# The start of the second layer's second job, the choice of its largest expert, and the turning of relu's values by halves

## The chip, the cores and the metric

The kernel runs on one core of one Trainium2 chip. The metric is device time in microseconds (us) of one execution, the median of several; lower is better.

## The reference

A retention attention over 1536 tokens (2 batches x 768) of 512 features is followed by two mixture-of-experts layers of 8 experts each, all in float32. The attention is not touched by the change. What the two layers compute, cut to what matters:

```python
# layer 1: noisy top-2 gating
noisy = x @ w_gate + log1p(exp(x @ w_noise)) * noise
top2, top2_w = two largest, softmax over them
out[mask] += top2_w[mask, k, None] * (np.maximum(x[mask] @ w1[e], 0.0) @ w2[e])

# layer 2: top-1 gating with a capacity of 384 tokens for each expert
logits = x @ w_gate
expert_idx = np.argmax(logits, axis=1)
gate_w = softmax(logits)[token, expert_idx]
# the first 384 tokens of an expert, in token order, are kept; others give 0
out[i] = gate_w[i] * (np.maximum(x[i] @ w1[e], 0.0) @ w2[e])
```

In both layers w1 is 512 x 1024 and w2 is 1024 x 512 for each expert.

## The kernel before

**Jobs.** The work of a layer is cut into jobs. A job is a set of token rows for one expert: the rows are gathered from memory by an indirect DMA on GpSimd's queue, transposed on TensorE, multiplied by w1, passed through relu, multiplied by w2, weighted and scattered. Layer 1 has two jobs begun ahead and then seven jobs of 372 to 408 rows. Layer 2 has job S (AHEAD, 256 rows of the largest expert, chosen while the last job of layer 1 still runs, from the tokens that job does not hold), job T (BEHIND, 128 more rows of the same expert, with S's weights), and then seven jobs, each for the expert of some rank by size, in the order TURNS = (336, 128, 324, 128, 164, 152, 128 rows). "Job 2" below is the first of these, with 336 rows in three gathers.

**Arithmetic.** Each product is made of three matmuls on high and low parts (`three`, L754 to L756). The weights' high part is cast by ScalarE (L106), the low part subtracted by VectorE (L112). Rows arrive as pairs that GpSimd adds (`both`, L514); TensorE transposes them (L744), ScalarE casts the high part (L745) and VectorE subtracts the low part (L746).

**Steps of a job.** `Job.steps` gives a list of steps. A wide job has nine: first product of one eighth of the hidden features (`first`, 12 matmuls) together with the second product of the eighth before (`second`, 12 matmuls; 6 in S). A job of one 128-row tile works "by token" and has four: `first_rows(0)` and `first_rows(1)` (24 matmuls each, of 128 x 256), whose relu goes to a tile `hr` (ScalarE, L843); `turn(0)` and `turn(1)`, in which TensorE transposes `hr` back, four 128 x 128 pieces each (L850), ScalarE copies the high part (L853) and VectorE subtracts the low part (L854); then `second` in two steps. Five jobs work by token: one of layer 1's first two, T, and the three of 128 rows in layer 2.

**Routing of layer 2.** `ahead` chooses the largest expert: logits are loaded (L1203) and added (L1206), ranked on TensorE (`ranks_of`, L300 and L303), and S's rows are found (`one_hot`, L374 to L387). While S runs, `extra2` routes the rest: `route2` and `one_hot("D", ...)` for T's rows; `others` (sizes, weight loads, and `slots`: `mark` writes twelve 128 x 128 comparisons on VectorE, L451, and `head` multiplies them on TensorE, L458, to give `Tsrc`, the rows of all seven later jobs); `gates` (softmax weights into `aux2`, L1300 to L1313 by way of `split3`, L309 to L313); then the products that bring each row its weight: `jobS.rest` and `jobT.rest` (24 matmuls at L377, copies L379, small transposes L382) and `later[1][7]` (12 matmuls at L458). `sizes_by_expert` and `leftovers` (L991 to L1002) count tokens that no job holds; a branch (L1391) reads that count.

**Order.** `experts` walks jobs and steps and calls `extra(j, i)` after step i of job j. Each engine executes its instructions in one order; `tc.issue_after(x)` keeps what is issued inside behind instruction x, and `tail["pe"]`, `tail["act"]` and `tail["dve"]` hold the latest of an engine. In between the scheduler places instructions by its own estimate. An instruction that waits holds all behind it on its engine. In `experts`, `last.collect()` and `last.finish()` (results of the job before, with its scatters on GpSimd) come after step 0 of a job.

Of the kernel before, what the change touches and what calls it, by code (L numbers as in the profile page):

```python
# [20 lines left out]
P = 128  # L21
# [5 lines left out]
AHEAD, BEHIND = (256, 2), (128, 1)  # L27
# [10 lines left out]
def kernel(ctx: ExitStack, tc: tile.TileContext, q, k, v, lam, g1, gn, noise,  # L38
                                  w1, w2, g2, u1, u2, capacity, out):
    nc = tc.nc  # L40
# [717 lines left out]
    class Job:  # L758
        def __init__(self, key, size, select, source, target, first_layer, wide=False, ranked=False):
            self.key, (self.n, self.nt), self.select = key, size, select  # L760
            self.ranked = ranked
            self.rows = P if ranked else self.n // self.nt
            self.source, self.target, self.first_layer = source, target, first_layer
            self.by_token = self.nt == 1
            self.wide = wide or self.nt > 2
            self.pairs = self.wide and 2 * self.n <= 512
            self.keeps = False
            self.g = self.logits = None
            self.yT = None
            self.apart = not first_layer  # L770
            self.h = {}
# [19 lines left out]
        def steps(self):  # L791
            if self.by_token:
                return [lambda: self.first_rows(0), lambda: self.first_rows(1),
                        lambda: (self.turn(0), self.turn(1), self.second(range(0, 4))),
                        lambda: self.second(range(4, FC))]
            return [lambda: self.first(0)] + [
                (lambda f: lambda: (self.first(f + 1) if f + 1 < FC else None, self.second((f,))))(f)
                for f in range(FC)]
# [34 lines left out]
        def first_rows(self, m):  # L833
            r = self.rows
            ps = bank("hp", [P, 512])[:r]
            for jj in range(2):
                for d in range(DC):
                    w = w1_part(self.key, 2 * m + jj, d, slice(0, 256))
                    three(ps[:, jj * 256:(jj + 1) * 256], (self.x[:, d, 0, :r], self.x[:, d, 1, :r]), w,
                          d == 0, d == DC - 1)  # L840
            used[0] += 2
            hr = work.tile([P, 512], F32, name="hr")
            nc.scalar.activation(hr[:r], ps, AF.Relu)  # L843
            self.h["r", m] = hr

        def turn(self, m):
            r = self.rows
            ps = bank("tr", [P, 4, P])[:, :, :r]
            for i in range(4):
                nc.tensor.transpose(ps[:, i, :], self.h["r", m][:r, i * P:(i + 1) * P], ident[:r, :r])  # L850
            t = work.tile([P, 2, 512], F32R, name="h", bufs=3).rearrange("p a (b c) -> p a b c", b=4)[:, :, :, :r]
            hh, hl = t[:, 0], t[:, 1]
            nc.scalar.copy(hh, ps)  # L853
            nc.vector.tensor_sub(hl, ps, hh.bitcast(F32))  # L854
            for i in range(4):
                self.h[4 * m + i] = t[:, :, i, :]
# [91 lines left out]
    def experts(jobs, last, extra=None, count=None, between=None, joins=3):  # L948

        j = 0  # L950
        while j < len(jobs) and j != count:
            job = jobs[j]
            steps = job.steps()
            for i, step in enumerate(steps):
# [3 lines left out]
                nxt = jobs[j + 1] if j + 1 < len(jobs) else None  # L958
                if i == len(steps) - 1 and j + 1 < len(jobs) and j + 1 != count:
                    job.collect()  # L960
                if i == 0 and last is not None:
                    last.collect()
                    last.finish()
                    if j == 0 and between is not None:
                        between()
# [176 lines left out]
    def extra1(j, i):  # L1142
# [14 lines left out]
        if j == len(FIRST) + 1:  # L1157
            if i == 0:
                final()
            if i == 2:  # L1160
                tokens_of(jobs[j])
                load_logits()
            if i == 4:
                last_logits(lgp)
                first_max(lgp, mm, mb2, sl)
                nc.vector.tensor_mul(mb2[:, sl], mb2[:, sl], whole[:, :, None].to_broadcast(full))
                ahead()
# [107 lines left out]
    keyB, keys, gate = (small(x, [P, NT]) for x in ("keyB", "keys", "gate"))  # L1275
    oo, mB = mb2[:, sl], mb1[:, sl]
    jobT = Job(("b", "s"), BEHIND, None, x2_rows, out, False)
    jobs = [jobS, jobT]
    entered2, regs, later = [], [], []
    tot2 = cnt2[:, NT, :]  # L1280
# [67 lines left out]
    def extra2(j, i):  # L1348
# [5 lines left out]
            later.append(picked)  # L1354
        if j == 0 and i == 3:
            with tc.issue_after(later[0]):
                rk2 = others()
                later.append(rk2)
                of, _, pick, spread1, mark, head = later[1][:6]
                pick()  # L1360
                spread1()
                mark(range(NT))
                later.append(head())
                for k, r in enumerate(TURNS):
                    jobs.append(Job(("b", r), SECOND[r], of(r), x2_rows, out, False, SECOND[r][1] > 1, True))
                jobs[2].prepare()
        if j == 0 and i == 4:
            st2 = sizes_by_expert("b", later[2], [n for n, _ in SECOND] + [BEHIND[0]])
            later.append(leftovers("b", tab2, table2_full, tot2, st2, x2_rows, u1, u2, out, False))

        if j == 0 and i == 5:
            with tc.issue_after(later[3]):
                gates()
            with tc.issue_after(tail["pe"]):
                jobS.rest()
                jobT.rest()
                later[1][6]()
                later[1][7]()
            places.append(more[2])

    jobL = last
    last = experts(jobs, jobL, extra2, count=BEFORE + 2, between=lambda: all_logits(jobL))
# [47 lines left out]
```

## Time and profile before

| what | us |
|---|---|
| median of 3 runs | 632.45 |
| the three runs | 632.22, 632.45, 636.45 |
| the profiled execution's own time | 632.51 |
| its span, first to last instruction | 630.8 |
| TensorE busy | 598.5 |
| VectorE busy | 373.1 |
| ScalarE busy | 279.8 |
| GpSimd busy | 180.1 |

The trace gives a start and a duration for each instruction. In its timeline a row may stand for several like instructions in turn (x3); a bracket at the end of a row tells how long the engine sat idle before it and which instruction, on which engine and line, ended that. Matmuls overlap, so what one costs is read from the distance of the starts. The attention fills the first 92 us, layer 1 goes on to about 423 us, S begins there, T stands at 461 us and job 2 at 476 us. L numbers are lines of the kernel before.

### The profile page before, as it was taken

The page shows a single profiled execution, that of the slowest core. Times are in us where ns is not written, and L with a number is a line of the kernel's source. Part 1 is how long each engine was busy: PE and PEld are TensorE (multiplying, and loading weights), DVE is VectorE, ACT ScalarE, POOL GpSimd, SP SyncE. Part 2 cuts the span into 40 slices and gives each one's busy share as a digit, 9 for nine tenths or more (in the row PEclk, how much of TensorE's full clock was granted, in tenths as well). Part 3 has the DMA queues.
Part 4 walks back from the last instruction along what each step waited for, and adds up shares of the span by engine and source line. Part 5 has one row for each costly group of instructions (what it writes and reads, how often), then busy time and mean ns, then how long its engine had stood idle before and what let it go on. Part 6 is the DMA issues. An engine that isn't in the chain of part 4 may idle for free. (4 is left out here: it accounts for less than half of the span.)

```text
span 630.8 us, 11323 instructions
## 1 busy us (share of the span) xinstructions
PE 598.5 (95%) x4173; PEld 558.7 (89%) x4173; DVE 373.1 (59%) x841; ACT 279.8 (44%) x486; POOL 180.1 (29%) x255
## 2 busy tenths in 40 slices
PE   3999989999999999999999999989899999998896
PEld 3888878989999999999999999978679989987795
DVE  3365769857454363554745535447859568557881
ACT  2466622146353353443534334145037367466771
POOL 3953730274022040120500101032255135132101
PEclk9999999999999999999999999999999999999999
DMA  6799721577645375476532511272597877767620
GB/s 151 156 302 266 186 82 44 168 215 254 203 144 170 109 232 151 136 221 200 193 113 100 177 44 55 60 251 85 171 324 239 277 240 259 248 201 246 214 75 34
DMA packets 106048, 110.34 MB, mean 175 GB/s; under 512 B 35855, under 2 KB 81951, under 8 KB 105984
## 3 DMA queue, kind: packets, MB, share of 16 engines
q1 hardware_dynamic: 97920, 83.58, 43.9%
q0 software_dynamic: 8064, 25.95, 12.2%
q8 instruction: 35, 0.57, 0.4%
q14 instruction: 29, 0.24, 0.1%
HBM read 92.48 MB, written 18.79 MB: 176 GB/s over the span
## 5 line engine op out<-in xcount | busy, mean ns | idle before, releaser
L112 DVE TENSOR_TENSOR wl<-wst,wh 128x1024 fp32r<-128x1024 f32 x107 | 135.2, 1270 | 59.0 <-ACT wh L106 58.6
L106 ACT CAST wh<-wst 128x1024 fp32r<-128x1024 f32 x107 | 111.3, 1047 | 33.4 <-PE yp L755 26.5
L754 PE MATMUL hp<-x,wh 128*128 128x372 f32 (+9 forms) x352 | 116.1, 330 | 0.8 <-ACTq L1264 0.4
L755 PE MATMUL hp<-x,wh 128*128 128x372 f32 (+9 forms) x352 | 116.1, 330 | 0.0
L756 PE MATMUL hp<-x,wl 128*128 128x372 f32 (+9 forms) x352 | 115.3, 328 | 0.0
L828 ACT ACTIVATE h<-hp 128x372 fp32r<-128x372 f32 (+9 forms) x88 | 41.2, 469 | 154.7 <-PE hp L756 151.6
L754 PE MATMUL yp<-h,wh 128*128 128x372 f32 (+8 forms) x320 | 106.9, 334 | 0.0
L756 PE MATMUL yp<-h,wl 128*128 128x372 f32 (+8 forms) x320 | 106.3, 332 | 0.0
L755 PE MATMUL yp<-h,wh 128*128 128x372 f32 (+8 forms) x320 | 105.8, 331 | 0.0
L829 DVE SCALAR_TENSOR_TENSOR h<-hp,h 128x372 fp32r<-128x372 f32 (+9 forms) x88 | 46.4, 527 | 62.9 <-ACT h L828 62.6
L754 PEld LDWEIGHTS hp<-x,wh 128*128 128x128 f32 x352 | 66.1, 188 | 1.9 <-ACTq L1264 0.7
L755 PEld LDWEIGHTS hp<-x,wh 128*128 128x128 f32 x352 | 66.2, 188 | 0.4
L756 PEld LDWEIGHTS hp<-x,wl 128*128 128x128 f32 x352 | 66.1, 188 | 0.1
L504 POOL DMA_INDIRECT xg<-x,Rsrc x25 | 26.4, 1057 | 136.0 <-PE tr L744 118.8
L755 PEld LDWEIGHTS yp<-h,wh 128*128 128x128 f32 x320 | 60.2, 188 | 0.6 <-DVE h L829 0.4
L756 PEld LDWEIGHTS yp<-h,wl 128*128 128x128 f32 x320 | 60.2, 188 | 0.2 <-issue 0.2
L754 PEld LDWEIGHTS yp<-h,wh 128*128 128x128 f32 x320 | 60.2, 188 | 0.0
L746 DVE TENSOR_TENSOR x<-tr,x 128x128 fp32r<-128x128 f32 (+12 forms) x72 | 29.2, 436 | 38.0 <-ACT x L745 37.5
L941 POOL DMA_INDIRECT x<-y,Rdst x25 | 25.0, 1000 | 80.9 <-DVE y L915 78.5
L745 ACT CAST x<-tr 128x128 fp32r<-128x128 f32 (+12 forms) x72 | 25.9, 387 | 41.3 <-PE tr L744 40.8
L514 POOL TENSOR_TENSOR xg<-xg 128x512 f32<-128x512 f32 (+1 forms) x16 | 24.7, 1546 | 39.3 <-DMA xg<-x,Tsrc 24.4
L906 PE MATMUL tr<-iw,yT 128*128 128x136 f32 (+2 forms) x224 | 34.2, 287 | 0.0
(370 smaller groups left out, 1029.3 us busy)
## 6 DMA issues: line engine op xcount, KB each, us to landing
wst<-in_moe_w_dram SPq DMA_DIRECT2D x107, 512.0 KB, 4.8
more<-in_moe_w_dram SPq DMA_DIRECT2D x21, 512.0 KB, 5.3
ldk<-in_k_dram SPq DMA_DIRECT2D x12, 256.0 KB, 5.5
ldq<-in_q_dram SPq DMA_DIRECT2D x6, 512.0 KB, 6.2
ldv<-in_v_dram SPq DMA_DIRECT2D x12, 256.0 KB, 6.0
x<-xr SPq DMA_DIRECT2D x12, 256.0 KB, 2.9
out_dram<-zero SPq DMA_DIRECT2D x12, 256.0 KB, 4.9
dm<-powers SPq DMA_DIRECT2D x1, 512.0 KB, 5.4
```

Of the source, the lines that this page charges most:

```text
L106: nc.scalar.copy(hi, st)
L112: nc.vector.tensor_sub(lo, st, hi.bitcast(F32))
L504: i = nc.gpsimd.indirect_dma_start(out=r, out_offset=None, in_=x, in_offset=bass.IndirectOffsetOnAxis(ap=src(s)[:m], axis=0))
L745: a = nc.scalar.copy(hi[:, d, :n], ps[:, :n])
L746: v_ = nc.vector.tensor_sub(lo[:, d, :n], ps[:, :n], hi[:, d, :n].bitcast(F32))
L754: nc.tensor.matmul(ps, a[0], b[0], start=start, stop=False)
L755: nc.tensor.matmul(ps, a[0], b[1], start=False, stop=False)
L756: tail["pe"] = nc.tensor.matmul(ps, a[1], b[0], start=False, stop=stop).ins
L828: tail["act"] = nc.scalar.activation(hh, ps, AF.Relu).ins
L829: tail["dve"] = nc.vector.scalar_tensor_tensor(hl, ps, 0.0, hh.bitcast(F32), op0=OP.max, op1=OP.subtract).ins
L906: nc.tensor.matmul(ps[:m, i, :], self.yT[:, 2 * b + i, s * r:s * r + m], iw[:, 2 * b + i, gates2], start=True, stop=True)
L941: i = nc.gpsimd.indirect_dma_start(out=target, out_offset=bass.IndirectOffsetOnAxis(ap=dst, axis=0), in_=y, in_offset=None, bounds_check=t ...
```

## The change

Three things are moved; TensorE's number of instructions stays as it was.

- In the last job of layer 1, the logits' sum, `first_max` and `ahead` come after step 3 instead of step 4.
- At layer 2's start, `head` of the later jobs' rows and the gather of job 2 come after S's step 7 instead of step 3. The gates come after them (step 7 instead of 5), the weights' products after T's step 0, sizes and leftovers after T's step 1. S's results are collected and scattered after T's step 1 (`clears = 1`).
- In a job by token, `turn(0)`'s transposes stand in the middle of `first_rows(1)`, and `turn(1)`'s after the first two of `second`'s eight parts.

```diff
         def steps(self):
             if self.by_token:
                 return [lambda: self.first_rows(0), lambda: self.first_rows(1),
-                        lambda: (self.turn(0), self.turn(1), self.second(range(0, 4))),
+                        lambda: (self.second(range(0, 2)), self.turn(1, tail["pe"]), self.second(range(2, 4))),
                         lambda: self.second(range(4, FC))]
...
             for jj in range(2):
+                if m and jj:
+                    self.turn(0, tail["pe"])
                 for d in range(DC):
...
-        def turn(self, m):
+        def turn(self, m, ahead):
             r = self.rows
             ps = bank("tr", [P, 4, P])[:, :, :r]
-            for i in range(4):
-                nc.tensor.transpose(ps[:, i, :], self.h["r", m][:r, i * P:(i + 1) * P], ident[:r, :r])
+            with tc.issue_after(ahead):
+                for i in range(4):
+                    nc.tensor.transpose(ps[:, i, :], self.h["r", m][:r, i * P:(i + 1) * P], ident[:r, :r])
...
-                if i == 0 and last is not None:
+                if i == job.clears and last is not None:
                     last.collect()
                     last.finish()
...
-            if i == 4:
+            if i == 3:
                 last_logits(lgp)
                 first_max(lgp, mm, mb2, sl)
...
+    jobT.clears = 1
...
         if j == 0 and i == 3:
             with tc.issue_after(later[0]):
-                rk2 = others()
-                later.append(rk2)
-                of, _, pick, spread1, mark, head = later[1][:6]
+                later.append(others())
+                of, _, pick, spread1, mark = later[1][:5]
                 pick()
                 spread1()
                 mark(range(NT))
-                later.append(head())
-                for k, r in enumerate(TURNS):
-                    jobs.append(Job(("b", r), SECOND[r], of(r), x2_rows, out, False, SECOND[r][1] > 1, True))
+        if j == 0 and i == 7:
+            with tc.issue_after(tail["pe"]):
+                later.append(later[1][5]())
+                for r in TURNS:
+                    jobs.append(Job(("b", r), SECOND[r], later[1][0](r), x2_rows, out, False, SECOND[r][1] > 1, True))
                 jobs[2].prepare()
-        if j == 0 and i == 4:
-            st2 = sizes_by_expert("b", later[2], [n for n, _ in SECOND] + [BEHIND[0]])
-            later.append(leftovers("b", tab2, table2_full, tot2, st2, x2_rows, u1, u2, out, False))
-
-        if j == 0 and i == 5:
-            with tc.issue_after(later[3]):
+        if j == 0 and i == 7:
+            with tc.issue_after(later[3]), tc.issue_after(tail["dve"]):
                 gates()
+                later[1][6]()
+        if j == 1 and i == 0:
             with tc.issue_after(tail["pe"]):
                 jobS.rest()
                 jobT.rest()
-                later[1][6]()
                 later[1][7]()
             places.append(more[2])
+        if j == 1 and i == 1:
+            with tc.issue_after(tail["dve"]):
+                st2 = sizes_by_expert("b", later[2], [n for n, _ in SECOND] + [BEHIND[0]])
+                later.append(leftovers("b", tab2, table2_full, tot2, st2, x2_rows, u1, u2, out, False))
```

TensorE's order in the middle of T, before (`hr` is relu's output, `hp` the first product's and `yp` the second product's bank, `iw` holds the identity matrix):

```order
L756 MATMUL hp<-wh_79,x_1224 128x256
L850 MATMUL tr<-iw,hr 128x128 x8
L754 MATMUL yp_5330<-wh_80,h 128x512
L755 MATMUL yp_5330<-wl_88,h 128x512
L756 MATMUL yp_5330<-wh_80,h 128x512
L754 MATMUL yp_5330<-wh_80,h 128x512
L755 MATMUL yp_5330<-wl_88,h 128x512
L756 MATMUL yp_5330<-wh_80,h 128x512
```

and of the change, the two places where four transposes each stand now:

```order
L756 MATMUL hp<-wh_78,x_1224 128x256
L854 MATMUL tr<-iw,hr 128x128 x4
L754 MATMUL hp<-wh_79,x_1224 128x256
...
L754 MATMUL yp_5322<-wh_80,h 128x512
L755 MATMUL yp_5322<-wl_88,h 128x512
L756 MATMUL yp_5322<-wh_80,h 128x512
L854 MATMUL tr<-iw,hr 128x128 x4
L754 MATMUL yp_5322<-wh_81,h 128x512
L755 MATMUL yp_5322<-wl_89,h 128x512
```

The eight transposes that stood together between the two products are now four among the first product's matmuls, twelve ahead of its end, and four behind six matmuls of the second. All five jobs by token have this order.

VectorE's order around the change from S to T, before (`Tsrc` are the later jobs' rows, `aux` the gates' split values, `tabi` the copy of the weights' products):

```order
L472 TENSOR_SCALAR Tsrc<-slt 128x21
L475 SCALAR_TENSOR_TENSOR Tdst<-slt,sld 128x21
L996 TENSOR_REDUCE blw<-ovs 128x8
...
L313 CAST aux_152<-sp_r 128x12
L446 TENSOR_TENSOR yT<-yT,aux_152 128x756
L379 COPY tabi<-tr 4x256
L383 COPY Soa<-tr 128x2x4
```

and of the change (`wl` is the low part of job 2's weights):

```order
L472 TENSOR_SCALAR Tsrc<-slt 128x21
L475 SCALAR_TENSOR_TENSOR Tdst<-slt,sld 128x21
L1305 TENSOR_REDUCE keeps<-keep 128x12
...
L313 CAST aux_152<-sp_r 128x12
L112 TENSOR_TENSOR wl_84<-wst_73,wh_76 128x1024
L446 TENSOR_TENSOR yT<-yT,aux_152 128x756
L112 TENSOR_TENSOR wl_85<-wst_74,wh_77 128x1024
L379 COPY tabi<-tr 4x256
```

Two conversions of job 2's weights now stand between the gates and the first copy of the weights' products.

GpSimd's order from the gather of T's rows on, before (`Dsrc` are T's rows, `Tsrc` those of job 2 and later, `Sdst` where S's results go):

```order
L504 DMA xg<-x_67,Tsrc 128x1104 x2
L504 DMA xg<-x_67,Tsrc 80x1104
L514 TENSOR_TENSOR xg<-xg 128x4x128 x2
L941 DMA out_dram<-y,Sdst 1536x512 x2
L514 TENSOR_TENSOR xg<-xg 80x4x128
L504 DMA xg<-x_67,Tsrc 128x1104
```

and of the change:

```order
L504 DMA xg<-x_67,Tsrc 128x1104 x2
L504 DMA xg<-x_67,Tsrc 80x1104
L514 TENSOR_TENSOR xg<-xg 128x4x128 x2
L504 DMA xg<-x_67,Tsrc 128x1104
L514 TENSOR_TENSOR xg<-xg 80x4x128
L945 DMA out_dram<-y,Sdst 1536x512 x2
```

The third addition for job 2 and the first gather for the job after it stand ahead of S's two scatters now.

## Rows read from the trace of the kernel before

**Rows 1.** Page, busy time, share of the span and instructions of each engine

```profile
PE 598.5 (95%) x4173; PEld 558.7 (89%) x4173; DVE 373.1 (59%) x841; ACT 279.8 (44%) x486; POOL 180.1 (29%) x255
```

**Rows 2.** Waits of TensorE over the span: sum in us, times, longest

```profile
PE tr L850 <- ACT hr L843: 1.3, 5, 0.3
```

**Rows 3.** Timeline, TensorE, 417 to 421 us: start, duration, instruction, idle before and releaser

```profile
417.79 0.33 PE L756 MATMUL yp<-h,wl 128*128 128x372 f32 x1
418.33 0.33 PE L744 MATMUL tr<-iw,xg 128*128 128x128 f32 x1 [0.22 <-POOL xg L514]
420.21 0.55 PE L744 MATMUL tr<-iw,xg 128*128 128x128 f32 x3 [1.54 <-POOLq L1264]
420.51 0.41 PE L754 MATMUL yp<-h,wh 128*128 128x372 f32 x1
```

**Rows 4.** Timeline, GpSimd, the second addition for S's rows

```profile
418.89 1.26 POOL L514 TENSOR_TENSOR xg<-xg 128x512 f32<-128x512 f32 x1 [0.61 <-DMA xg<-x,Ssrc]
```

**Rows 5.** Timeline, VectorE, two steps' relu and the logits, 389 to 398 us

```profile
389.63 0.55 DVE L829 SCALAR_TENSOR_TENSOR h<-hp,h 128x372 fp32r<-128x372 f32 x1 [0.56 <-ACT h L828]
393.71 0.55 DVE L829 SCALAR_TENSOR_TENSOR h<-hp,h 128x372 fp32r<-128x372 f32 x1 [3.54 <-ACT h L828]
396.10 0.26 DVE L1206 TENSOR_TENSOR lgp<-lg 128x96 f32<-128x96 f32 x1 [1.84 <-DMA lg<-x]
...
397.85 0.26 DVE L1166 TENSOR_TENSOR mb<-mb,whole 128x96 bf16<-128x96 bf16 x1
```

**Rows 6.** Timeline, TensorE, the ranks for the largest expert

```profile
403.21 0.22 PE L300 MATMUL tr<-mb,tri 128*128 128x104 bf16 x1
```

**Rows 7.** Timeline, TensorE, from S to T's first matmul

```profile
453.32 0.47 PE L458 MATMUL yp<-yT,more 128*128 128x42 bf16 x12 [1.60 <-DVE more L451]
...
455.87 0.73 PE L756 MATMUL yp<-wh,h 128*128 128x512 f32 x2 [0.42 <-DVE h L829]
457.82 1.47 PE L377 MATMUL tr<-oh,aux 128*4 128x256 bf16 x12 [1.23 <-DVE aux L313]
...
461.72 0.39 PE L754 MATMUL hp<-wh,x 128*128 128x256 f32 x1 [0.40 <-ACT x L745]
```

**Rows 8.** Tile `more`, group of the marks' comparisons: duration ns min/median/max, first and last start

```profile
L451 DVE TENSOR_SCALAR more<-slot,yT x36: 242/245/1352, 114.1 to 453.0; 128x128 bf16<-128x128 f16 x36
```

**Rows 9.** Timeline, GpSimd, additions for T's rows and job 2's second and third gather

```profile
451.79 1.26 POOL L514 TENSOR_TENSOR xg<-xg 128x512 f32<-128x512 f32 x1 [3.78 <-DMA xg<-x,Dsrc]
...
465.57 1.99 POOL L514 TENSOR_TENSOR xg<-xg 128x512 f32<-128x512 f32 x1 [1.32 <-DMA xg<-x,Tsrc]
...
470.85 1.32 POOL L514 TENSOR_TENSOR xg<-xg 80x512 f32<-80x512 f32 x1
```

**Rows 10.** Timeline, TensorE, T's turn and the start of its second product

```profile
467.78 0.28 PE L756 MATMUL hp<-wh,x 128*128 128x256 f32 x1
467.90 0.60 PE L850 MATMUL tr<-iw,hr 128*128 128x128 f32 x4
...
470.29 0.40 PE L754 MATMUL yp<-wh,h 128*128 128x512 f32 x1
...
472.35 0.74 PE L744 MATMUL tr<-iw,xg 128*128 128x128 f32 x6
...
473.21 0.40 PE L755 MATMUL yp<-wl,h 128*128 128x512 f32 x1
```

**Rows 11.** Timeline, ScalarE, the turned values' copy in T

```profile
469.50 0.59 ACT L853 CAST h<-tr 128x512 fp32r<-128x512 f32 x1 [0.32 <-PE tr L850]
```

**Rows 12.** Timeline, VectorE, the turned values' low part in T

```profile
470.12 0.69 DVE L854 TENSOR_TENSOR h<-tr,h 128x512 fp32r<-128x512 f32 x1 [0.21 <-ACT h L853]
```

**Rows 13.** Page, costliest groups: busy us, mean ns, idle before and what ended it

```profile
L112 DVE TENSOR_TENSOR wl<-wst,wh 128x1024 fp32r<-128x1024 f32 x107 | 135.2, 1270 | 59.0 <-ACT wh L106 58.6
L106 ACT CAST wh<-wst 128x1024 fp32r<-128x1024 f32 x107 | 111.3, 1047 | 33.4 <-PE yp L755 26.5
```

**Rows 14.** Windows: us, busy of PE, PEld, DVE, ACT, POOL, PEclk, DMA share, GB/s

```profile
455.00:460.00 5.00, 3.35 (x28) 2.06 (x27) 3.89 (x15) 0.28 (x1) 2.84 (x3) 1.00 1.07 380
```

More of the change, by code (lines that the diff above doesn't have):

```diff
@@ L767, in __init__ @@
             self.keeps = False
+            self.clears = 0
             self.g = self.logits = None
```

## The prediction

> **What bounds the kernel now.** I read the page's busy times first. TensorE is busy for 598.5 of 630.8 us [rows 1]; no other engine comes near. So the time is TensorE's work plus the moments at which it has nothing to do, and an edit is worth what it takes from either. The second view is the list of TensorE's waits: most are outside the reach of this change, and the ones within reach are few. Its row for the turn of relu's values is 1.3 us in five times [rows 2], one for each job by token. The others I take from TensorE's timeline, where a bracket shows what ended a wait: 0.22 and 1.54 us before the transposes of S's rows [rows 3]; then 1.60 us for the marks, 0.42 for the low part of relu, 1.23 for the gates' last split value and 0.40 for T's rows, all between S and T [rows 7]. After them I read the other engines at those moments, to see what would come late if TensorE came sooner.
>
> The sum is made in the profiled execution: it took 632.51 us, 1.71 more than its span, and the median is 632.45, so no correction is needed.
>
> **Choosing sooner.** From the last matmul before S's transposes to the first one behind them is 420.51 - 417.79 = 2.72 us [rows 3]. One matmul's place there is about 0.17 (a step of 24 matmuls takes 393.71 - 389.63 = 4.08 us [rows 5]), and four transposes cost about 0.46 (worked out under the turn). So 2.1 us are lost, and the 1.54 of them ends when GpSimd's second addition ends, at 418.89 + 1.26 = 420.15 [rows 4]. The choice comes one step, 4.08 us, sooner, so this addition would end at 416.1, ahead of TensorE at about 418. Is there data for it? The logits land at 396.1, the marks of the largest are there at 397.85 + 0.26 = 398.1 [rows 5], and TensorE ranks them only at 403.21 [rows 6]; a step sooner is 399.1, 1.0 us after. The cover is 1.0 us: if it went, VectorE would hold TensorE's ranks for the rest. All that ahead() issues moves with it, S's gathers and weight loads too; GpSimd and the load queue have nothing else there. A conversion of S's weights comes before the branch instead of after, which is ScalarE's and VectorE's time. I take 1.85 us (2.1 less some 0.25 for transposes of the last job's results that now stand closer); bounds 0 and 2.1.
>
> **The start of T.** TensorE's work is the same, so I count waits. Gone from where they are: 1.60 + 0.42 + 1.23 + 0.40 = 3.65 us [rows 7]. What is late next:
> - The marks. TensorE now comes to their products six matmuls after relu instead of four, and with two transposes of T's rows between: some 0.7 us later. VectorE does the marks behind less other work, but one of them took 1.352 us instead of 0.245 [rows 8] at the time of GpSimd's addition for T (451.79, 1.26 us [rows 9]), and that meeting stays. I leave 0.2 of the 1.60; bounds 0 and 0.9.
> - The gates. T's first product starts where the old waits and the products at L377 and L458 are not: these fill 461.72 - 0.40 - 457.82 = 3.5 us, so it starts near 461.72 - 3.65 - 3.5 + 0.5 = 455.1 on the old clock (0.5 for T's own transposes), and its 24 matmuls of 0.12 us (467.90 - 467.78 [rows 10]) end at 458.0. The gates' last value is there at 457.8 before [rows 7]. I take 0.3, in case of delays by the memsets and counts of the leftovers that stand among the gates now; bounds 0 and 1.
> - The copy of the weights' products (L379). It now stands behind two conversions of job 2's weights, 1.27 us each [rows 13], which themselves wait for casts of 1.05. TensorE has the 12 products at L458 (0.47 for such a group [rows 7]) and seven matmuls of 0.12 between, 1.3 us. I take 0.25; bounds 0 and 2.5, the two conversions whole.
>
> That is 3.65 - 0.75 = 2.9 us. Then T's end: TensorE comes sooner to the transposes of job 2's rows. Before, they stand at 472.35 [rows 10], and GpSimd's third addition ends at 470.85 + 1.32 = 472.17 [rows 9]: they are just in time. The change puts this addition ahead of S's scatters (it could follow the second, 465.57 + 1.99 = 467.56 [rows 9], and end near 468.9). TensorE's new time is 472.35 - 2.9 - 0.76 (T's turn, below) = 468.7. So it is just in time again: I take a wait of 0.3, bounds 0 and 1.8 (one addition of 1.99 instead of 1.28 or so, and one more blocked). Sum of this part: 2.6 us, bounds -1.8 and 3.65.
>
> The slow mark stands in a rule: the Trainium skill, "SBUF — State Buffer", section "Who interferes with whom", says that VectorE and GpSimd share a port pair that one instruction holds whole, so that the other blocks until it is done; the trace agrees in one case, by 1.352 - 0.245 = 1.1 us, near the 1.26 of the addition. It speaks against the change: additions for job 2 meet conversions with two inputs in memory. If each of its three additions cost the later engine one such 1.1 us on the path, the sum would be lower by 3.3; I keep the bounds above, since most conversions don't hold TensorE.
>
> **The turn.** Before, eight transposes stand together, TensorE waits 0.26 for the second relu (1.3 us in five [rows 2]), and the second product's third matmul waits for the low part. From 467.90 to the fourth matmul at 470.29 is 2.39 us [rows 10]; three matmuls at 0.229 (nine from 470.29 to 472.35 [rows 10]) are 0.69, so the turn costs 1.70. Among matmuls, six transposes cost 473.21 - 472.35 - 0.229 = 0.63 [rows 10]; I take 0.47 for four, so 0.94 for both halves. A job saves 0.76, and five jobs 3.8 us. What hides the copies: after the first four transposes, 12 matmuls of 0.12 and two of the second product, 1.44 + 0.46 = 1.9 us, stand before the low part is wanted. The copy takes 0.59 [rows 11] and the subtraction 0.69, and VectorE waited 0.21 before it [rows 12]; twice that for the passing between engines makes 1.7. It is covered by little. A conversion of 1.05 on ScalarE stands just ahead of the copy [rows 13], in place of the wait. I take off 0.05 a job: 3.55 in all; bounds 1.5 (0.45 a job lost) and 3.9.
>
> **Sum.** 1.85 + 2.6 + 3.55 = 8.0 us; 632.5 - 8.0 = 624.5 us. All parts at their good end give 2.1 + 3.65 + 3.9 = 9.65, so 622.8; lower still, 622, if transfers that start sooner also shorten waits after T.
>
> **Rivals.**
> 1. GpSimd or its transfers become the new wait at job 2. For it: a DMA share of 1.07 at 455 to 460 us [rows 14], when these gathers are on their way: the 16 engines are full, so rows can't come sooner. Against it: the queue of additions is shorter by two scatters. Then TensorE waits about 1.8 us at job 2 and the neighbour's conversions lose 0.5: 624.5 + 2.3 = 626.8.
> 2. The weights' products only move their waits: VectorE's two conversions ahead of L379 hold TensorE for 2.5 us, and part two is worth 0.35. For it: the order; against it: TensorE's 1.3 us of other work, half of the two conversions. Time 624.5 + 2.25 = 626.75.
> 3. The choice isn't sooner where it counts, since the logits' transfer (the 1.84 us wait ending at 396.10 [rows 5]) decides. For it: that wait; against it: 1.0 us of margin. Time 624.5 + 1.85 = 626.35.
> 4. Slower: ScalarE. The copy of the first half stands behind a cast of weights that must have landed; before, the transposes came later by the whole of 1.4 us. If the casts of the next job's weights wait for their load, TensorE stops in the middle of each job by token. It decides where a load comes over 2 us late in each of the five: at 2 us the turn's 3.55 becomes 3.55 - 10 and the time 634.5. For it: the full DMA engines [rows 14]; against it: the casts' idle time is nearly all put down to TensorE's use of the slots (26.5 of 33.4 us), not to a transfer [rows 13].
>
> **How the numbers follow.** Forecast 0.60, rival 1 0.15, rival 2 0.12, rival 3 0.07, rival 4 0.06. A measurement of this kernel can tell about 1% (6.3 us) from no change. Below 626.1 lies the forecast's case but for a tenth of it, and half of rivals 1 to 3, whose times are within a microsecond of that line: 0.54 + 0.17 = 0.71, less a little for two at once: 0.68. Within 1% the rest, but 0.03 for the part of rival 4 beyond 638.8. The range goes from 622.0 to 628.0, which takes in rivals 1 to 3 with a second small loss, and leaves out rival 4 and sums of several.
>
> **What would show it.** In the changed profile, S's four transposes should have no wait of over 0.3 us, and the last addition for S should end before 416. Between S and T's first matmul there should be one wait of under 1 us, and waits at L377, L382 and L458 of under 1 us together. No wait of TensorE for `hr`; T's second product begins after 24 + 24 matmuls without a gap, and job 2's first matmul stands near 471 us. If the waits between 450 and 470 add up to over 3 us, part two was wrong; if the wait at L744 for GpSimd is over 1.5 us, rival 1; if the second product waits for the low part by over 0.3 us in each job by token, the turn's cover was too thin; if the relu of the steps at 390 to 400 us comes late, rival 3.

## The result and the profile after

The changed kernel took 624.59 us (median of 4 runs, 623.98 to 626.13), the kernel before 632.71 beside it: a ratio of 0.9876, 95% interval 0.9853 to 0.9899. That is 8.1 us less; 8.0 were forecast, and 624.5 as the time. The sum came out right, but not all of its terms did, and that they cancelled to 0.1 us is luck. The profiled execution was the longest of the four (626.13 us, span 624.4), and why it was is part of the story.

The table gives the stages of three profiles as distances, in us, between the starts of TensorE's first matmuls. The third column is a second profile of the changed kernel (run f1 below).

| from the first matmul of ... to ... | before | changed | changed, second profile |
|---|---|---|---|
| layer 1 to the job behind its job by token | 50.42 | 49.63 | 49.69 |
| that job to S | 278.60 | 276.65 | 276.63 |
| S to T | 37.97 | 30.82 | 30.75 |
| T to job 2 | 14.74 | 20.88 | 19.51 |
| job 2 to the second job by token of layer 2 | 30.28 | 30.13 | 30.13 |
| this job (128 rows) | 15.81 | 14.96 | 14.96 |
| the job of 324 rows | 29.31 | 29.31 | 29.08 |
| the next job of 128 rows | 16.02 | 15.24 | 15.23 |
| the jobs of 164 and 152 rows | 43.62 | 43.61 | 43.56 |
| the last job, to the last matmul's end | 13.91 | 13.17 | 13.17 |

The weights' products moved from S's stage to T's, so these two rows are to be read as a sum: 52.71 before, 51.70 and 50.26 after.

On the page of the changed kernel TensorE is busy for 2.0 us less than in [rows 1]:

```profile
PE 596.5 (96%) x4173; PEld 560.6 (90%) x4173; DVE 370.8 (59%) x841; ACT 280.7 (45%) x486; POOL 181.6 (29%) x255
```

TensorE's waits between 390 and 480 us. The waits of [rows 3] and [rows 7] are gone but for 0.2 us at the marks' product, and one is new, the first; the 0.4 us at L754 stands before S's first matmul in both kernels:

```profile
PE tr L744 <- POOL xg L514: 2.1, 1, 2.1
PE hp L754 <- ACTq L1268: 0.4, 1, 0.4
PE yp L458 <- DVE more L451: 0.2, 1, 0.2
```

S's transposes in TensorE's timeline, which answer to [rows 3]: eight in all, with no bracket, among the last job's matmuls.

```profile
417.29 0.60 PE L744 MATMUL tr<-iw,xg 128*128 128x128 f32 x4
...
418.59 0.44 PE L744 MATMUL tr<-iw,xg 128*128 128x128 f32 x2
...
419.04 0.38 PE L744 MATMUL tr<-iw,xg 128*128 128x128 f32 x2
```

From T's first matmul to its second product, against [rows 7] and [rows 10]. T begins straight behind S, the weights' products follow its first 24 matmuls, and four transposes cost 459.73 - 459.37 = 0.36 us plus 0.09 on the next matmul:

```profile
451.70 0.28 PE L754 MATMUL hp<-wh,x 128*128 128x256 f32 x1
...
454.63 1.47 PE L377 MATMUL tr<-oh,aux 128*4 128x256 bf16 x12
...
458.12 0.28 PE L382 MATMUL tr<-iw,tabi 4*128 4x4 f32 x2
...
459.37 0.60 PE L854 MATMUL tr<-iw,hr 128*128 128x128 f32 x4
459.73 0.36 PE L754 MATMUL hp<-wh,x 128*128 128x256 f32 x1
...
462.63 0.60 PE L854 MATMUL tr<-iw,hr 128*128 128x128 f32 x4
```

Then the new wait. GpSimd's timeline (against [rows 9]) has the third gather for job 2, the three additions, and between the second and third of them the gather for the job behind job 2:

```profile
454.55 1.90 POOL L504 DMA_INDIRECT xg<-x,Tsrc  x1 [0.30 <-issue]
459.61 1.29 POOL L514 TENSOR_TENSOR xg<-xg 128x512 f32<-128x512 f32 x1 [3.16 <-DMA xg<-x,Tsrc]
463.51 1.28 POOL L514 TENSOR_TENSOR xg<-xg 128x512 f32<-128x512 f32 x1 [2.62 <-DMA xg<-x,Tsrc]
464.94 0.95 POOL L504 DMA_INDIRECT xg<-x,Tsrc  x1
465.91 1.28 POOL L514 TENSOR_TENSOR xg<-xg 80x512 f32<-80x512 f32 x1
```

TensorE wants these rows at 464.46 and gets the last of them at 465.91 + 1.28 = 467.19:

```profile
464.46 0.71 PE L744 MATMUL tr<-iw,xg 128*128 128x128 f32 x2
467.25 0.95 PE L744 MATMUL tr<-iw,xg 80*128 80x80 f32 x4 [2.07 <-POOL xg L514]
467.93 0.78 PE L754 MATMUL yp<-wh,h 128*128 128x512 f32 x1
468.50 0.63 PE L755 MATMUL yp<-wl,h 128*128 128x512 f32 x1
```

TensorE's idle time by the bracket is 2.07 us; from 464.46 to 467.25 are 2.79 us, where two transposes otherwise take 0.22, so 2.6 us are lost by the starts.

The last two rows stand 0.57 us apart instead of 0.32 (a matmul behind transposes), and those after them 0.43 instead of 0.23. The windows of this stretch show why (us, busy of PE, PEld, DVE, ACT, POOL, granted clock, DMA share, GB/s): the granted clock is 0.52 behind the wait, mostly the lower of its two levels, 1.2 instead of 2.4 GHz.

```profile
465.00:467.00 2.00, 0.18 (x1) 0.00 (x0) 0.00 (x0) 0.00 (x0) 1.98 (x2) 0.98 0.94 296
467.00:470.50 3.50, 3.25 (x12) 2.77 (x13) 1.02 (x2) 0.88 (x2) 2.87 (x4) 0.52 0.71 271
470.50:475.00 4.50, 4.50 (x28) 4.13 (x27) 3.38 (x4) 3.68 (x6) 3.29 (x4) 1.00 0.41 119
```

### The profile page after: what moved, and what is told of

Its sections match the earlier page's. It is cut to its first block, busy times and chain, and to the rows that moved or that the text cites. A ratio compares the mean times of both kernels' runs of the same rounds, so it can differ in the third digit from the quotient of the medians.

```text
span 624.4 us, 11317 instructions
## 1 busy us (share of the span) xinstructions
PE 596.5 (96%) x4173; PEld 560.6 (90%) x4173; DVE 370.8 (59%) x841; ACT 280.7 (45%) x486; POOL 181.6 (29%) x255
## 5 line engine op out<-in xcount | busy, mean ns | idle before, releaser
L754 PE MATMUL hp<-x,wh 128*128 128x372 f32 (+9 forms) x352 | 116.4, 331 | 0.8 <-ACTq L1268 0.4
L754 PE MATMUL yp<-h,wh 128*128 128x372 f32 (+8 forms) x320 | 106.9, 334 | 0.0
L754 PEld LDWEIGHTS hp<-x,wh 128*128 128x128 f32 x352 | 66.1, 188 | 2.0 <-ACTq L1268 0.7
L504 POOL DMA_INDIRECT xg<-x,Rsrc x25 | 27.8, 1112 | 134.9 <-PE tr L744 117.6
L754 PEld LDWEIGHTS yp<-h,wh 128*128 128x128 f32 x320 | 60.2, 188 | 0.0
```

The costliest lines, as they stand in the source:

```text
L504: i = nc.gpsimd.indirect_dma_start(out=r, out_offset=None, in_=x, in_offset=bass.IndirectOffsetOnAxis(ap=src(s)[:m], axis=0))
L754: nc.tensor.matmul(ps, a[0], b[0], start=start, stop=False)
```

## The experiments

My theory after the profiles of the kernel before and of the changed one: the choice and the turn give what they should, each by itself; the new start of T gives most of its gain back at job 2's rows, because TensorE now comes there ahead of GpSimd, and in the first profile the lower clock took more. The rivals: the start is worth all that was forecast and the first profile was a bad execution; or the wait is of GpSimd's queue alone, not of the rows' transfer.

**The three parts apart.** Run e1 is the kernel before with the choice a step sooner, e2 with the turn in halves, e3 with the new start alone, e4 with choice and turn. All four stood beside one kernel before (632.37 us).

```diff
# e1 (and e4): on the kernel before
-            if i == 4:
+            if i == 3:
                 last_logits(lgp)
```

> Only the sooner choice of the largest expert, on the kernel before. My theory, from the landmarks of the two profiles (S's first matmul 2.87 us sooner, 0.92 of it from layer 1's job by token): 1.95 us less, ratio 0.997; S's transposes without a wait; the ranks at L300 follow S's logits by some 0.3 us. Rival (the logits' transfer decides): ranks wait and the gain is under 1 us.

Measured: 629.65 us, ratio 0.9958 (0.9943 to 0.9972). Its transposes for S have no wait:

```profile
418.62 0.60 PE L744 MATMUL tr<-iw,xg 128*128 128x128 f32 x4
```

S comes 276.44 instead of 278.60 us after the job behind layer 1's job by token: 2.16 us. The ranks came without a wait for the logits, so the rival falls. The gain of 2.7 us in the medians is more than that: S's own stage is 0.64 us shorter too (37.33 for 37.97). One conversion of its weights is now done before it begins (three instead of two), which may be the reason; no run tried that alone.

```diff
# e2 (and e4): steps, first_rows and turn as in the change, on the kernel before
-                        lambda: (self.turn(0), self.turn(1), self.second(range(0, 4))),
+                        lambda: (self.second(range(0, 2)), self.turn(1, tail["pe"]), self.second(range(2, 4))),
```

> Only the turn in two halves, on the kernel before. My theory: 0.79 us for each job by token, but T's is lost, since in the kernel before GpSimd's third addition for job 2 ends only 0.18 us before TensorE wants it: 4 x 0.79 + 0.2 = 3.4 us less, ratio 0.9947, with a new wait of about 0.6 us at L744 in T. Rival (the five are independent and job 2's rows don't matter): 3.95 us less, ratio 0.9938, no wait at L744.

Measured: 628.69 us, ratio 0.9953 (0.9936 to 0.9969), so 3.7 us. Four of the five jobs by token are shorter by 0.77, 0.87, 0.78 and 0.75 us; T by 0.21 only. So T's share is lost, as I expected, but not where I expected it: no transpose of job 2's rows waits. What T waits for is the low part of the turned values:

```profile
PE yp L756 <- DVE h L857: 0.3, 1, 0.3
```

By the starts this costs 0.5 us. ScalarE's copy of these values ended at 465.86, but VectorE was in a conversion of job 2's weights until 466.72 (its row below). The limit that I had expected stands right behind it: GpSimd's third addition ends at 470.24, and TensorE's transposes begin at 470.25.

```profile
465.17 1.55 DVE L112 TENSOR_TENSOR wl<-wst,wh 128x1024 fp32r<-128x1024 f32 x1 [0.68 <-PE tr L853]
```

```diff
# e3: the change with the choice at step 4 and the turn as before
-            if i == 3:
+            if i == 4:
                 last_logits(lgp)
...
-                        lambda: (self.second(range(0, 2)), self.turn(1, tail["pe"]), self.second(range(2, 4))),
+                        lambda: (self.turn(0), self.turn(1), self.second(range(0, 4))),
```

> Only the new start of T and job 2, on the kernel before. My theory (the part's gain is given back at job 2's rows): T's first matmul 7 to 8 us sooner after S's start, but T's transposes of job 2's rows wait 1.3 us or more for GpSimd, so 1.0 to 1.6 us less than before, ratio 0.9975 to 0.9985; with the lower clock behind the wait as in the changed kernel, nothing is left. Rival (the part is worth what the prediction said and the profiled execution was a late one): 2.6 us less, ratio 0.996, and a wait under 0.5 us.

Measured: 630.75 us, ratio 0.9977 (0.9965 to 0.9989), so 1.6 us. The wait at job 2's rows is there:

```profile
471.28 0.58 PE L744 MATMUL tr<-iw,xg 80*128 80x80 f32 x4 [1.58 <-POOL xg L514]
```

S and T together take 51.34 instead of 52.71 us, 1.37 less. T begins 31.76 us after S, 6.2 sooner and not 7 to 8, partly because its own rows now wait 0.75 us. The rival's 2.6 us and its wait under 0.5 us are not what the run shows.

> The sooner choice and the turn, without the new start of T. My theory: 1.95 + 3.4 = 5.35 us less, ratio 0.9915; against the changed kernel's 0.9876 the new start is then worth 2.5 us only together with the others. If the new start gives back everything, this kernel is as fast as the changed one (0.9876 to 0.990).

Measured: 625.68 us, ratio 0.9897 (0.988 to 0.9914), so 6.7 us, more than the 5.35 expected, since both parts gave more alone as well (2.7 for 1.95 and 3.7 for 3.4); they add up to 6.4. Nothing shows that the two parts depend on each other. Beside the changed kernel's 0.9876 (0.9853 to 0.9899) the start adds some 1.3 us to them, about what it gives alone, though these intervals overlap. In the profiles S and T together take 51.85 us here, 51.70 and 50.26 us in the two of the changed kernel. The start's gain is all but gone where the clock falls, and half of the 3.3 us forecast (2.6 and T's turn) where it stays.

**What makes the wait.** Four kernels beside one kernel before (632.21 us): the changed one again (f1); one in which GpSimd's gather for the job behind job 2 is held behind the third addition (f2); one in which two of the seven weight loads for job 2 are held (f3); and both (f4). In f3 two of the buffers that the loads fill are given out only behind small reads on VectorE after the weights' products. Five loads then go out ahead of the gathers, as before; the sixth and the seventh go at 455.91 and 457.90, into buffers that VectorE's conversions free, instead of at 448.45 and 449.02 (the changed kernel).

> The changed kernel itself, for the comparison with the three kernels beside it on one chip. My theory: ratio to before 0.9876 as first measured, TensorE waits about 2 us at L744 for GpSimd's third addition for job 2, and its clock goes down to half behind that wait for some 3.5 us. If the first profile was a late execution, the wait is under 1 us here and the clock stays.

Measured: 624.20 us, ratio 0.9871 (0.9841 to 0.99). The wait is the same as in the first profile, but the clock stays up (windows, columns as above):

```profile
467.05 0.58 PE L744 MATMUL tr<-iw,xg 80*128 80x80 f32 x4 [2.06 <-POOL xg L514]
```

```profile
466.00:468.00 2.00, 0.95 (x7) 0.86 (x8) 0.15 (x1) 0.62 (x2) 1.83 (x2) 1.00 0.92 281
```

By the starts 2.6 us are lost here too (464.22 to 467.05). So the wait belongs to the kernel and the fall of the clock to some executions of it. T's stage is 19.51 us here and 20.88 in the first profile: the lower clock cost 1.4 us there. This is most of the 1.8 us between the two profiled executions' times (624.32 and 626.13).

```diff
# f2 (and f4): on the change, in Job.prepare
-                self.g = gather(self.src, self.n, self.rows, self.source)
+                with tc.issue_after(tail["both"]) if self.key == ("b", TURNS[1]) else ExitStack(): self.g = gather(self.src, self.n, self.rows, self.source)
```

> The gather for the job after job 2 is held behind GpSimd's third addition for job 2. My theory (GpSimd's order makes half of the wait): the third addition begins 0.97 us sooner, the wait falls from 2.07 to about 1.1 us and, if the clock stays up, TensorE also keeps the 1.2 us it lost behind the wait: 1.0 to 2.2 us faster than the changed kernel, ratio to before 0.984 to 0.986. Rival (the rows' transfer alone decides): the third addition waits for its rows instead and nothing is gained.

Measured: 624.09 us, ratio 0.9863 (0.9834 to 0.9892): by the times no different from f1. In the trace the third addition comes sooner, but then waits for its rows, and TensorE's idle time falls by 0.5 us, half of what I expected (GpSimd's row, then TensorE's):

```profile
465.03 1.26 POOL L514 TENSOR_TENSOR xg<-xg 80x512 f32<-80x512 f32 x1 [0.63 <-DMA xg<-x,Tsrc]
```

```profile
466.35 0.58 PE L744 MATMUL tr<-iw,xg 80*128 80x80 f32 x4 [1.56 <-POOL xg L514]
```

T's stage is 18.60 us, 0.9 less than in f1. The second addition too comes 0.4 us sooner after T's first matmul than in f1, where TensorE had a wait of 0.18 for it; the edit does not touch that addition, so not all of the 0.9 is the gather's.

```diff
# f3 (and f4): on the change
     def others():
-        places.extend(more[:2])
         id2, rk2 = by_size("b", tot2, isA)
...
                 later[1][7]()
-            places.append(more[2])
+                held = small("held", [P, 2])
+                for k in range(2):
+                    nc.vector.tensor_add(held[:, k:k + 1], more[k][:, :1], jobs[2].wt(0))
+            places.extend(more)
```

> Two of the seven weight loads for job 2 are held until the weights' products are done, some 6 us behind the gathers; two small reads on VectorE do that. My theory (the rows share the DMA engines with the loads): 1 MB less ahead of the rows, at 380 GB/s up to 2.7 us sooner, so the second addition begins about 2 us sooner and the wait at L744 shrinks from 2.07 to under 0.5 us: 1.5 to 3 us faster than the changed kernel, ratio to before 0.983 to 0.985. Rival (GpSimd's queue decides): second addition sooner, but the wait stays above 1.5 us.

Measured: 622.93 us, ratio 0.9843 (0.9814 to 0.9871); 1.3 us less than f1, a little under what I expected. The rows land 5.6 us after their gathers were issued instead of 10.1 (median of the three gathers for job 2; first the changed kernel, then f3):

```profile
xg<-x,Tsrc POOLq DMA_INDIRECT x3, 10.1
```

```profile
xg<-x,Tsrc POOLq DMA_INDIRECT x3, 5.6
```

In the first 5 us or so behind their issue the gathers' queue (packets, MB, share of the DMA engines; changed kernel from 451.5 to 457, then f3 from 452 to 457) moves 0.11 MB beside 1.95 MB of the loads, and 0.68 beside 1.25 in f3:

```profile
q0 software_dynamic: 26, 0.11, 5.5%
```

```profile
q0 software_dynamic: 168, 0.68, 35.3%
```

The issue of the third gather takes 1.89 us here as in f1, so that is not the difference. The first two additions then stand together, the second 4.6 us sooner after T's first matmul than in f1, and although the third is behind S's scatters again, it starts at 464.19, ahead of TensorE (GpSimd's rows of f3, then TensorE's, which has no bracket any more):

```profile
457.84 2.63 POOL L514 TENSOR_TENSOR xg<-xg 128x512 f32<-128x512 f32 x2 [1.16 <-DMA xg<-x,Tsrc]
...
464.19 1.32 POOL L514 TENSOR_TENSOR xg<-xg 80x512 f32<-80x512 f32 x1
```

```profile
465.39 0.75 PE L744 MATMUL tr<-iw,xg 128*128 128x128 f32 x6
```

T's stage is 17.57 us, 1.9 less than in f1. The loss of 2.6 us is gone, but TensorE comes to the rows 0.7 us later after T's first matmul than in f1: VectorE's first small read and an instruction for S's weights behind it (L399) take 0.77 and 1.16 us beside GpSimd's two additions, and ScalarE's copy of the first turned half stands behind one that waits for these weights. This decides between the two: the rows' transfer behind the weight loads is the larger part of the wait. Its size is not explained in full: 1 MB less ahead of the rows was to give 2.7 us, and they came 4.5 sooner.

> Both edits together. My theory: no wait at L744 and no fall of the clock, 3.2 us faster than the profiled execution of the changed kernel, ratio to before 0.982 to 0.984. If the two are the same gain, it is no better than the better of them.

Measured: 623.01 us, ratio 0.9847 (0.982 to 0.9874), T's stage 17.50 us and no wait at the rows. It is the same gain as f3's, as the second half of the expectation has it.

**Fewer loads, and once more.** Three kernels beside one kernel before. All of them took some 10 us longer in this comparison, the kernel before too (642.49 us); the profiles of the three put this into layer 1's job by token (the table's first stage is 59.2 to 59.4 us), so only ratios and later stages are used.

```diff
# h1: as f3, but one load is held
-        places.extend(more[:2])
+        places.extend(more[:1])
...
-            places.append(more[2])
+                nc.vector.tensor_add(small("held", [P, 1]), more[1][:, :1], jobs[2].wt(0))
+            places.extend(more[1:])
```

> One of the seven weight loads is held behind the weights' products instead of two. My theory (bytes ahead of the rows set the second addition's start): 0.5 MB less, so the second addition begins some 1.5 to 2 us sooner than the changed kernel's 463.4 and the wait at L744 falls from 2.1 to 0.5 to 1.3 us; TensorE's time from T's first matmul to job 2's lies between 17.6 (two held) and 19.5 us (none), near 18.5. Rival (a single late load decides): all of the gain or none of it.

Measured: ratio 0.9863 (0.9838 to 0.9888). The second addition begins 9.2 us after T's first matmul, between f1's 11.8 and f3's (its two additions fill 457.84 to 460.47, so some 7.2): 2.6 us sooner for one load, more than the 1.5 to 2 expected. But the wait stays at 1.6 us and T's stage at 19.49, where 18.5 was expected, because the third addition now stands behind a gather and S's two scatters, which fill GpSimd's time from 471.4 to 474.95 (TensorE's waits, then GpSimd's third addition):

```profile
PE tr L744 <- POOL xg L514: 1.6, 1, 1.6
PE tr L382 <- DVE tabi L379: 0.6, 1, 0.6
```

```profile
474.96 1.29 POOL L514 TENSOR_TENSOR xg<-xg 80x512 f32<-80x512 f32 x1
```

So GpSimd's queue is the other limit: with the rows there early, the place of the third addition in it, and the time at which the second ends, decide.

> The changed kernel once more, for the spread of its profile: wait at L744 2.1 us again, and T's first matmul to job 2's 19.5 us if the clock stays up, 20.9 if it falls behind the wait. Ratio to before 0.987.

Measured: ratio 0.9869 (0.9849 to 0.9889); wait 2.07 us, and the clock falls behind it, to 0.60 over this window. T's stage is 21.31 us, 0.4 above the expectation; it has waits at L382 of 0.6 us besides.

```profile
476.50:480.80 4.30, 3.50 (x13) 2.94 (x14) 1.01 (x2) 1.03 (x3) 3.63 (x4) 0.60 0.74 263
```

> Two loads held, once more beside the changed kernel: no wait at L744, T's first matmul to job 2's 17.6 us, 1.3 to 2 us faster than the changed kernel. If the first comparison was luck, the two are within 0.5 us.

Measured: ratio 0.985 (0.9822 to 0.9879), medians 633.90 against 634.62 for h2: 0.7 us, less than the 1.3 expected. There is no wait at job 2's rows, as in f3, but one of 2.0 us at the copy of the weights' products, so T's stage is 20.01 us. VectorE's row shows the conversion ahead of that copy late, by ScalarE, and long, 2.10 us instead of 1.22; GpSimd's first addition for job 2 had begun 0.25 us before it (VectorE's row, then GpSimd's):

```profile
PE tr L382 <- DVE tabi L379: 2.0, 1, 2.0
```

```profile
467.25 2.10 DVE L112 TENSOR_TENSOR wl<-wst,wh 128x1024 fp32r<-128x1024 f32 x1 [1.09 <-ACT wh L106]
```

```profile
467.00 1.28 POOL L514 TENSOR_TENSOR xg<-xg 128x512 f32<-128x512 f32 x1 [2.11 <-DMA xg<-x,Tsrc]
```

This is the prediction's second rival, in one execution of another kernel. ScalarE's first relu of T began 4.55 us after T's first matmul, and 3.9 in h1 and h2 instead of 3.0 in the first profile. So ScalarE was late in all three kernels here, in h2 with no load held; the cause is open. The addition met the conversion because the rows had landed sooner and the conversion came later; in f3 it began as the conversion ended (457.84 and 456.66 + 1.22). So these 0.9 us come of both, the held loads and the late ScalarE. Over the two comparisons f3 and h3 have the lowest ratios, 0.9843 and 0.985 against 0.9871 and 0.9869; the wait's absence is plain in all three profiles with two loads held, while the difference in time lies within the intervals.

## Why the prediction was right

The forecast of 624.5 us met 624.59, by terms that were partly off and made up for each other. The choice and the turn are right in mechanism and size. The start of T was forecast 0.9 us too good, by two errors of 1.4 and 2.3 us in opposite directions.

- **Choosing sooner**, forecast 1.85: 1.95 us in the changed kernel's stage up to S, 2.16 alone. The mechanism is as told: TensorE's wait for GpSimd's addition went, and the margin of 1.0 us for the logits held. The addition itself moved less than told: in e1 it ended 2.4 us sooner, not 4.08 (417.77 for 420.15), since S's rows took 7.4 us from their gather to the first addition instead of 5.9. In the changed kernel it ended at 414.01 + 2.64 = 416.65, not before 416, and TensorE came at 417.29, so this cost nothing (GpSimd's row):

```profile
414.01 2.64 POOL L514 TENSOR_TENSOR xg<-xg 128x512 f32<-128x512 f32 x2 [4.63 <-DMA xg<-x,Ssrc]
```

  That S's own stage became shorter as well, by 0.64 in e1, I had not counted.
- **The turn**, forecast 0.71 a job: 0.79, 0.85, 0.78 and 0.74 in the four jobs outside T. I had left 0.05 a job for the low part; in these jobs it costs nothing. Rival 4, ScalarE's copy behind a cast, doesn't show in any of the four.
- **The start of T: the waits on the way.** Forecast 0.75 us left of 3.65 (0.2 at the marks, 0.3 at the gates, 0.25 at the copies). In the changed kernel's first profile 0.2 at the marks is all that is listed. So this term was 0.5 too high, and rival 2 didn't come about in it. The 3.65 us themselves were sized by the brackets, while the other parts go by distances of starts, and here the two differ: from the matmul before each of the four waits to the one behind it are 1.99, 0.82, 1.62 and 0.72 us, where neighbours mostly stand 0.23 apart or less. That is some 4.2 us. The rows of those matmuls, in the kernel before:

```profile
451.33 0.40 PE L755 MATMUL yp<-wl,h 128*128 128x512 f32 x1
...
455.05 0.40 PE L755 MATMUL yp<-wl,h 128*128 128x512 f32 x1
...
456.20 0.40 PE L756 MATMUL yp<-wh,h 128*128 128x512 f32 x1
...
461.00 0.33 PE L744 MATMUL tr<-iw,xg 128*128 128x128 f32 x1
```

- **The start of T: job 2's rows.** Here the prediction's step failed in size: a wait of 0.3 us (bounds 0 and 1.8) was 2.07, above the 1.5 that the prediction named as rival 1's sign; by the starts 2.6 were lost, and the fall of the clock added 1.4 in the first profile. The step was "it could follow the second, 465.57 + 1.99 = 467.56, and end near 468.9". Two things were wrong with it. The order printed ahead of the prediction has a gather between the second and the third addition, 0.97 us, and I passed over it (in f2, without it, TensorE's idle time is 0.5 shorter, since the third rows come no sooner). And I let the rows land where they did before, while they took 10.1 us instead of 9.1 (median of the three gathers), again behind seven weight loads. TensorE was moreover 1.4 us sooner there than I had it: 464.46 - 420.88 = 43.6 us after S's first matmul, where 468.7 - 423.75 makes 45.0: 0.55 by the waits on the way and some 0.55 by the brackets above; the other 0.3 isn't settled. Rival 1, at 0.15, is thus what happened at this place, and its price of 2.3 us was about right; its time of 626.8 was missed because TensorE had gained more on the way.
- **The sum.** In the second profile the stages give 0.73 + 1.97 + 2.45 up to job 2 and 2.82 behind it, 7.97 us, against 8.0. S and T together gave 0.86 less than forecast (2.45 for 2.6 and T's turn of 0.71): TensorE came to job 2's rows 5.1 us sooner after S's first matmul (43.5 for 48.6) instead of 3.65, and lost 2.6 us there instead of 0.3. The choice gave 0.12 more, the four other turns 0.27 more (3.11 for 2.84), and the stages that the change doesn't touch 0.44 (30.28, 29.31 and 43.62 became 30.13, 29.08 and 43.56). In the first profile the clock took 1.4 us of it, and 6.3 were left; the job of 324 rows lacks 0.2 more.
- **The port rule.** The sum by it would have been 3.3 us worse, one blocked instruction of 1.1 us for each addition for job 2. The additions took 1.29, 1.28 and 1.28 us, so none was held up, and no wait of TensorE is put down to one that a conversion blocked. What was held up is the issue of the third gather, below. In h3 a conversion was held up, by 0.9 us beside an addition, straight ahead of the copy that TensorE waited for; so this price can come on the path, though not three times.

## What to carry to other kernels

When a stage is made to start sooner, the transfers for the stage after it don't come sooner by themselves: look at what stands ahead of them in the DMA engines, and at every instruction between them and their user in the issuing engine's order. Here bulk loads that were wanted later had been put ahead of small gathers that were wanted at once, and holding two of them took away the wait. A wait's bracket is not what the wait costs: here four waits of 3.65 us cost some 4.2 by the starts, and one of 2.07 cost 2.6. And a term that comes out "just in time" should be given a wide price on one side only, since what comes early gains nothing and what comes late costs its whole lateness, and at times the clock too.

## What the runs showed of the hardware

The same wait at the same place let the clock fall in two of three profiled executions of one kernel (2.07 us with a fall in the first profile and in h2, 2.06 us without one in f1), and in e3 a wait of 2.35 us in front of S's transposes did not. So one profile doesn't tell what such a wait costs: the fall added 1.4 us in the first profile, and nothing in f1.

The issue of the third gather took 1.90 us in the changed kernel and 0.91 in h3. VectorE's conversion beside it began at 454.44 in the first, 0.11 us ahead of the gather, and at 464.09 in the second, 0.11 behind it. In f1 to f4, h1 and h2 the conversion began 0.11 to 0.12 ahead, and the issue took 1.89 (VectorE's row of the changed kernel, then GpSimd's and VectorE's of h3):

```profile
454.44 1.22 DVE L112 TENSOR_TENSOR wl<-wst,wh 128x1024 fp32r<-128x1024 f32 x1
```

```profile
463.98 0.91 POOL L504 DMA_INDIRECT xg<-x,Tsrc  x1 [0.30 <-issue]
```

```profile
464.09 1.21 DVE L112 TENSOR_TENSOR wl<-wst,wh 128x1024 fp32r<-128x1024 f32 x1
```

The Trainium skill, "SBUF — State Buffer", section "Who interferes with whom", holds that the order of issue decides which of the two engines is blocked. For the gather the rows agree. For the conversion they show nothing of the kind: with the gather ahead of it, in h3, it took 1.21 us, and 1.22 in the changed kernel.

The 10 us in layer 1's job by token, in the comparison of h1 to h3, hit all the kernels there. The trace of h1 puts 4.8 us of it before a matmul for which TensorE waited for nothing that the profile shows, and the clock is at its lower level behind it (0.50 from 140 to 145 us). In h2 the same wait, 4.1 us, is put down to ScalarE's copy of the turned values:

```profile
PE yp L754 <- issue: 4.8, 1, 4.8
```

```profile
PE yp L754 <- ACT h L857: 4.1, 1, 4.1
```

ScalarE stood idle for 7.76 us before that copy in h1, 6.38 in h2 and 6.37 in h3, where f1 has 0.79, and the traces of the three name only "remote" as what released it. So ScalarE was late first, there as in T; what held it is open.
